# Issuing a kernel's first loads in the program's first block, ahead of the entry barrier

## The chip, the cores and the metric

The kernel runs on one core of one Trainium2 chip. The metric is the device time of one execution in microseconds (us). A profile of one execution gives the span of the core, which is 1.3 to 1.8 us shorter than the device time in the runs here, and the record of each instruction and of each DMA packet. The time axis of a profile starts at the first recorded instruction.

Abbreviations of the profile: PE is TensorE (matmul), PEld its weight loads, DVE VectorE, ACT ScalarE, POOL GpSimd, SP SyncE. A "q" behind a name (SPq) is that engine's instruction sequencer, which also issues DMAs.

## The reference

One decoding step: pre-layernorm attention over a cache of 4096 keys, 32 heads, batch 4, then a dense block with a Mish activation. Everything is bf16.

```python
def _A_ref(x, k_cache, v_cache, wq, wo):            # x: 4 x 1 x 640
    q = (x @ wq).reshape(4, 1, 32, 128)...          # k_cache, v_cache: 4 x 32 x 4096 x 128
    scores = jnp.einsum("bhqd,bhkd->bhqk", q, k_cache) * (128 ** -0.5)
    p = _softmax(scores, axis=-1)
    o = jnp.einsum("bhqk,bhkd->bhqd", p, v_cache)
    return o...reshape(4, 1, 32 * 128) @ wo

h  = x + _A_ref(_layernorm(x), k_cache, v_cache, wq, wo)
h2 = h + _B_ref(_layernorm(h), w1, b1, w2)          # w1: 640 x 1728, b1: 1728, w2: 1728 x 640
```

The two caches are 268 MB, and each byte is used once.

## The kernel before

The work is cut into 16 tiles (`NT`) of 8 heads of one batch entry. A K tile and a V tile are 8 MB each. There are three big buffers, slots A, B and C; K tiles go to A and B, V tiles to C and A. wq sits in slot C at first, the later weights go into A and B at the end. SP issues nearly all loads; ScalarE issues four small ones. Each engine's program is written out with its own semaphore waits (`need`).

These are the loads that the change moves:

```python
    def first_loads():
        load(
            sp, slot["C"][:, 0 : DC * H * Dh], A_wq.rearrange("(p c) n -> p (c n)", c=DC), "wq", "WQ"
        )                                                            # 5 MB
        load(ac, x_bf[:, :], x_rows[:, :], "x", "X")                 # 5 KB
        load(ac, w2_tail[0:FT, :], B_w2[FM * P : F, :], "w2t", "WT") # 80 KB: rows 1664 to 1727 of w2
        k_load(0)                                                    # 8 MB into slot A
        k_load(1)                                                    # 8 MB into slot B
```

The end of SP's program and the start of ScalarE's, which the argument needs too:

```python
    def sync_prog():
        ...                                  # K and V tiles, each when its slot comes free
        sp.need(("F", NT - 1, NS - 1))       # slot B free
        for n, (q, j0, j1) in enumerate(WOS):
            load(sp, wo_sb[:, q, j0:j1, :], ..., ("wo", q, j0), f"W{n}")    # five pieces
        for k, (c0, c1) in enumerate(zip(W1S, W1S[1:])):
            load(sp, w1_sb[:, c0:c1, :], ..., ("w1", c0), ...)              # three pieces
        sp.need(("PV", NT - 2))              # slot A free
        for k, (j0, j1) in enumerate(zip(W2S, W2S[1:])):
            load(sp, w2_sb[:, j0:j1, :], ..., ("w2", j0), ...)              # four pieces
        ...
    def act_prog():
        ac.need("b1z")
        load(ac, b1T[:, 0:FM], ..., "b1a", "S")              # 3.2 KB, runs of 26 bytes
        load(ac, b1T[0:FT, FM : FM + 1], ..., "b1b", "S")    # 0.1 KB, runs of 2 bytes
        ...
```

And how the program is put together. Ahead of all this stands a first block, "main": four small memsets on GpSimd, then on each engine a drain and a semaphore wait that together make the entry barrier, then a branch to the next block.

```python
    with tc.tile_critical(name="k", no_gpsimd_drain=True):
        first_loads()
    tc.close()
    tc.compile()
    for p, f in progs:
        f()
        if p is po:
            clear()
```

The softmax here doesn't subtract the row's maximum and nothing guards it: scores larger than these inputs give would overflow.

Of the kernel before, what the change touches and what calls it, by code (L numbers as in the profile page):

```python
# [78 lines left out]
def kernel(  # L79
# [13 lines left out]
    nc = tc.nc  # L93
# [155 lines left out]
    def load(p, dst, src, key, sem):  # L249
        p.do(lambda: p.eng.dma_start(out=dst, in_=src), key, sem, 16)  # L250
# [15 lines left out]
    def clear():  # L266
        fin = book.handles["FIN"]
        nc.gpsimd.wait_ge(fin, 2).then_inc(fin, -2)
        nc.clear_and_free_semaphores(
            [h for k, h in book.handles.items() if k not in ("OUT0", "OUT1", "FIN")]  # L270
        )

    def k_load(i):
        c = KS[i % N]
        load(sp, slot[c][:, :], tiles(A_k_cache, i), ("K", i), "K" + c)
# [11 lines left out]
# [4 lines that stand above are left out]
        load(ac, x_bf[:, :], x_rows[:, :], "x", "X")  # L291
        load(ac, w2_tail[0:FT, :], B_w2[FM * P : F, :], "w2t", "WT")
        k_load(0)
        k_load(1)
# [654 lines left out]
    book.ready = True  # L949
    for p, f in progs:  # L950
        p.restart(True)
    with tc.tile_critical(name="k", no_gpsimd_drain=True):
        first_loads()
    tc.close()
    tc.compile()
    for p, f in progs:
        f()
        if p is po:
            clear()
# [30 lines left out]
```

## Time and profile before

The time before is 663.92 us (median of 3 runs, 663.88 to 663.99). What matters of its profile:

| quantity | value |
|---|---|
| span | 662.2 us |
| bytes in SP's DMA queue | 283.27 MB |
| share of that queue's packets in sixteen DMA engines' span | 99.0% |
| VectorE, TensorE busy | 61%, 60% |
| SP's first DMA issue | 0.95 us |
| first packet of that queue (packet records) | 1.96 us |
| last weights packet (packet records) | 658.1 us |

The queue table of before follows; its columns are packets, megabytes and share of sixteen engines' span. q1 is SP's queue, q10 ScalarE's; "..." marks lines left out, here and in all fences below.

```profile
q1 hardware_dynamic: 6640, 283.27, 99.0%
...
q10 hardware_dynamic: 328, 0.09, 0.1%
```

The first microseconds of before, from the timeline. The columns are start in us, duration in us, then the engine, source line and operation; the bracket is the idle time before it and what ended it.

```profile
0.90 0.56 ACTq L250 DMA_DIRECT2D x_bf<-in_A_x_dram  x1
0.95 0.40 SPq L250 DMA_DIRECT2D slotC<-in_A_wq_dram  x1
...
1.50 0.53 ACTq L250 DMA_DIRECT2D w_tail<-in_B_w_dram  x1
...
3.38 0.20 POOL L335 MEMSET ident<- 128x128 bf16 x1 [2.93 <-POOLq L955]
...
3.45 0.88 DVE L441 BATCH_NORM_STATS2 stats<-x_bf 4x6 f32<-4x320 bf16 x2
...
16.97 4.46 PE L708 MATMUL red<-slotC,lnT 128*32 128x512 bf16 x40 [8.54 <-PEq L49]
...
36.84 4.43 DVE L515 TENSOR_TENSOR slotA<-slotA,q_bc 128x8192 bf16<-128x8192 bf16 x1 [28.68 <-DMA slotA<-in_A_k_cache_dram]
```

SP could not issue before 0.95 us. TensorE had nothing to do between the end of its setup, about 8.4 us, and 16.97 us, when wq had landed. SP's own waits in before say what it stood at (columns: microseconds in total, times, longest); line 974 is the entry barrier:

```profile
SPq L974 <- PEq L974: 0.7, 1, 0.7
SPq L955 <- PEq L955: 0.5, 2, 0.3
```

The chain of waits of before, its first pieces in order of time (start, duration, what): it starts at the second half of the last V tile. "issue" is time in which the engine waited for nothing that the profile shows.

```profile
635.98 0.04 issue
636.02 3.60 PE pv L708 x30
639.62 1.69 PE y_ps L708 x40
...
645.90 1.55 PE y_ps L708 x40
647.46 0.04 issue
647.50 1.75 PE y_ps L708 x40
```

### The profile page before, as it was taken

How to read it: one execution, taken by the hardware profiler on the slowest of the kernel's cores; microseconds unless marked ns; L12 is line 12 of the kernel's file. 1: busy time of each engine (PE TensorE's matmuls, PEld its weight loads, DVE VectorE, ACT ScalarE, POOL GpSimd, SP SyncE). 2: the span in 40 equal slices, each digit the busy share in tenths (PEclk: the TensorE clock that was granted, in tenths of full speed). 3: DMA queues.
4: the chain of work that ended last, by engine and by line, in shares of the span. 5: the costliest groups of instructions: out<-in, count | busy, mean ns of one | idle time of the engine just before them, and what ended most of it. 6: DMA issues, size and time to landing. Idle time of an engine off the chain costs nothing. (4 is left out here: it accounts for less than half of the span.)

```text
span 662.2 us, 5205 instructions
## 1 busy us (share of the span) xinstructions
PE 399.4 (60%) x2747; PEld 83.3 (13%) x1787; DVE 406.8 (61%) x252; ACT 41.6 (6%) x158; POOL 2.6 (0%) x14
## 2 busy tenths in 40 slices
PE   0957666557317595838307485828534757675877
PEld 0710010101101010101100010100110001010147
DVE  1067889486048778677219688948306798858612
ACT  0110000000000000000000000000000000000011
POOL 1000000000000000000000000000000000000000
PEclk9998698869659796869668778977965879786855
DMA  9999999999999999999999999999999999999997
GB/s 385 437 443 413 420 444 433 444 435 436 421 432 439 428 443 435 439 420 435 439 428 435 443 439 420 435 439 424 439 439 443 420 435 435 428 439 439 412 419 289
DMA packets 6978, 283.50 MB, mean 428 GB/s; under 512 B 1012, under 2 KB 1208, under 8 KB 2232
## 3 DMA queue, kind: packets, MB, share of 16 engines
q1 hardware_dynamic: 6640, 283.27, 99.0%
q8 instruction: 7, 0.11, 0.1%
q10 hardware_dynamic: 328, 0.09, 0.1%
q14 instruction: 3, 0.02, 0.0%
HBM read 283.35 MB, written 0.01 MB: 428 GB/s over the span
## 5 line engine op out<-in xcount | busy, mean ns | idle before, releaser
L515 DVE TENSOR_TENSOR slotA<-slotA,q_bc 128x8192 bf16<-128x8192 bf16 x32 | 140.6, 4415 | 108.1 <-DMA slotA<-in_A_k_cache_dram 108.1
L515 DVE TENSOR_TENSOR slotB<-slotB,q_bc 128x8192 bf16<-128x8192 bf16 x32 | 140.7, 4417 | 17.0 <-DMA slotB<-in_A_k_cache_dram 17.0
L526 DVE TENSOR_REDUCE s_f<-red 128x64 f32<-128x1024 f32 x64 | 78.0, 1219 | 97.6 <-PE red L718 97.6
L718 PE MATMUL red<-slotA,ident 128*128 128x512 bf16 x480 | 135.9, 446 | 0.0
L718 PE MATMUL red<-slotB,ident 128*128 128x512 bf16 x480 | 127.9, 426 | 0.0
L708 PE MATMUL red<-slotA,ident 128*128 128x512 bf16 x32 | 14.3, 447 | 117.2 <-PEq L49 117.2
L708 PE MATMUL pv<-slotC,e 128*32 128x512 bf16 x768 | 53.1, 437 | 37.0 <-PEq L49 34.0
L708 PE MATMUL red<-slotB,ident 128*128 128x512 bf16 x32 | 14.1, 441 | 87.7 <-PEq L49 87.7
L394 ACT ACTIVATE ex<-s_f 128x64 bf16<-128x64 f32 x64 | 16.4, 256 | 503.2 <-DVE s_f L526 503.2
L540 DVE TENSOR_TENSOR e<-ex,hmask 128x512 bf16<-128x512 bf16 x64 | 39.8, 683 | 0.0
L708 PEld LDWEIGHTS pv<-slotC,e 128*32 128x32 bf16 x768 | 22.7, 108 | 94.1 <-issue 80.5
L708 PEld LDWEIGHTS red<-slotA,ident 128*128 128x128 bf16 x32 | 3.2, 99 | 184.7 <-issue 184.6
L708 PEld LDWEIGHTS red<-slotB,ident 128*128 128x128 bf16 x32 | 3.2, 99 | 171.9 <-issue 171.9
L708 PEld LDWEIGHTS o_ps<-pv_sb,selo 128*32 128x32 f32 x136 | 13.9, 113 | 65.0 <-issue 64.8
L708 PE MATMUL o_ps<-pv_sb,selo 128*32 128x128 f32 x136 | 18.9, 284 | 0.0
L708 PE MATMUL pv<-slotA,e 128*32 128x512 bf16 x256 | 14.6, 380 | 0.3 <-PEq L49 0.3
L404 ACT COPY pv_sb<-pv 128x512 f32<-128x512 f32 x16 | 9.4, 586 | 68.4 <-PE pv L708 68.4
L708 PE MATMUL red<-q_all,sel 32*128 32x128 bf16 x128 | 12.5, 307 | 0.8 <-PEq L49 0.8
L708 PEld LDWEIGHTS red<-q_all,sel 32*128 32x128 bf16 x128 | 12.2, 142 | 1.7 <-issue 1.7
L394 ACT ACTIVATION_READ_ACCUMULATOR ex<-s_f 128x1 f32 x64 | 11.9, 186 | 0.0
L708 PEld LDWEIGHTS pv<-slotA,e 128*32 128x32 bf16 x256 | 6.7, 97 | 23.4 <-issue 17.5
L708 PE MATMUL red<-slotC,lnT 128*32 128x512 bf16 x40 | 4.5, 629 | 8.5 <-PEq L49 8.5
(96 smaller groups left out, 74.3 us busy)
## 6 DMA issues: line engine op xcount, KB each, us to landing
slotC<-in_A_v_cache_dram SPq DMA_DIRECT2D x2, 4096.0 KB, 39.1
slotC<-in_A_wq_dram SPq DMA_DIRECT2D x1, 5120.0 KB, 15.9
slotB<-in_A_wo_dram SPq DMA_DIRECT2D x3, 1280.0 KB, 15.7
slotB<-in_B_w_dram SPq DMA_DIRECT2D x2, 864.0 KB, 22.8
slotB<-in_A_wo_dram SPq DMA_DIRECT2D x1, 960.0 KB, 20.1
slotA<-in_B_w_dram SPq DMA_DIRECT2D x1, 960.0 KB, 25.1
slotA<-in_B_w_dram SPq DMA_DIRECT2D x1, 640.0 KB, 22.3
slotB<-in_B_w_dram SPq DMA_DIRECT2D x1, 432.0 KB, 24.2
```

Of the source, the lines that this page charges most:

```text
L394: lambda: a.activation(out=ex[:, sl], in_=s_f[:, sl], func=ACT.Exp, scale=SCALE, accum_out=rs[:, b, s : s + 1],),
L404: lambda: a.copy(out=pv_sb[:, :, :].rearrange("p r d -> p (r d)"), in_=pv[:, :]),
L515: lambda: v.tensor_tensor(out=t, in0=t, in1=q_bc[:, hg, b, :].unsqueeze(1).to_broadcast([P, RS, Dh]), op=ALU.mult,),
L526: lambda: v.tensor_reduce(out=s_f[:, s * RS : (s + 1) * RS], in_=red[:, k : k + 2, :].rearrange("p k (r c) -> p (k r) c", c=CW), axis=AX.X ...
L540: lambda: v.tensor_tensor(out=e[:, sl, :], in0=ex[:, sl].unsqueeze(2).to_broadcast([P, RS, G]), in1=hmask[:, :].unsqueeze(1).to_broadcast( ...
L708: lambda: nc.tensor.matmul(out_, lhsT=lhsT, rhs=rhs, start=start, stop=stop, skip_group_check=skip),
L718: return t.add_instruction(mybir.InstMatmult(name=nc.get_next_instruction_name(), engine=mybir.EngineType.PE, ins=[t.lower_ap(rhs), t.lowe ...
```

## The change

The intent is to start the stream of loads sooner. The five first loads leave the critical section (`tile_critical`, a block that the other engines wait behind), which is dropped. They are issued after the program has been compiled, cut out of the block they fell into, and put into the block "main", on each engine just ahead of its drain, so that no barrier stands before them.

```diff
     for p, f in progs:
         p.restart(True)
-    with tc.tile_critical(name="k", no_gpsimd_drain=True):
-        first_loads()
     tc.close()
     tc.compile()
+    here = nc.cur_bb.bb
+    n = len(here.instructions)
+    first_loads()
+    moved = here.instructions[n:]
+    here.instructions = here.instructions[:n]
+    main = nc.bb_map["main"].bb
+    order = main.instructions
+    for ins in moved:
+        place = next(
+            k for k, o in enumerate(order) if o.engine == ins.engine and isinstance(o, mybir.InstDrain)
+        )
+        order = order[:place] + [ins] + order[place:]
+    main.instructions = order
     for p, f in progs:
         f()
```

## The prediction

> **What bounds the kernel now.** The SP DMA queue. Its packets take 99.0% of sixteen engines' span (queue table): 283.27 MB, mean 428 GB/s (DMA summary). In the packet records at least one packet of that queue is in flight at every moment from about 2.0 to 658.1 us, without a gap over 50 ns. VectorE is 61% and TensorE 60% busy, and VectorE's longest wait is for K tiles (108.1 us in four waits, waits table). The steady slices run at up to 444 GB/s; "DMA: Bandwidth & Descriptors" of the Trainium skill (section Specifications) puts the fabric ceiling at 435 GB/s, and this trace agrees within 2%. So transfers can't be made faster; they can start earlier. The chain of waits is the last 24 us of compute (636.0 to 660.3 us), which starts when the second half of the last V tile has landed, so it hangs on the stream too. The last weights land at 658.1 us, 1.9 us before the last matmul ends.
>
> **What the change does.** Timeline of the first 4 us: SP's first instruction, its drain, is at 0.00 us; it waits 0.7 us for the entry barrier (SP's wait table), passes a no-op and a branch, and issues wq at 0.95, K tile 0 at 1.40, K tile 1 at 1.87 us (0.40 to 0.42 us each). The first packet follows the first issue by 1.0 us. ScalarE's drain is at 0.14, its first issue at 0.90 us. After the change these issues stand ahead of the drain: SP should issue wq at about 0.0, ScalarE x at about 0.14 us. The critical section goes, with its branches, no-ops and two further barriers, which now let the compute engines begin at 3.4 us.
>
> Added: the entry barrier waits until SP has issued three transfers, 3 x 0.42 + 2 x 0.06 = 1.4 us, so the engines start at about 1.8 us (estimate from these durations), still 1.6 us sooner. That is off the critical path: TensorE finishes its setup at 8.4 us and waits until 16.94 us for wq.
>
> **How much is on the critical path.** Only the 0.95 us by which SP's first issue moves. Nothing should eat it: the queue is never empty later, since tiles are issued one or two ahead (27 to 45 us from issue to landing), and the releases that trigger them come from landings and shift with them. The matmuls on wq should start at 16.0 instead of 16.94, the first multiply at 35.9 instead of 36.84, the chain at 635.1 instead of 636.0; the span goes from 662.2 to 661.2.
>
> The tail runs at a granted clock of 0.50 from 630.5 us on. The clock changes in steps of 3.41 us; by "TensorE: Matmul & The Clock Gate" (section What's actually happening) that window is free-running, so a shift under 1 us lands nowhere in particular on it. Three runs of before agree within 0.11 us: I expect no luck from there.
>
> **Prediction.** 663.92 - 0.95 = 662.97 us, say 663.0; eight in ten between 662.3 and 663.8. Faster by over 2%: 0.005; within 2%: 0.99; slower: 0.005.
>
> **What would show it.** Right: SP issues at 0.0 / 0.45 / 0.9 us; first packet at about 1.05 us; VectorE's first instruction near 1.8 us; first matmul on wq near 16.0 us; unchanged GB/s in steady slices; a tail of 24 us. Wrong: an unchanged first packet (queue not ready earlier); a gap in the DMA records later; a longer tail, or one at another clock.
>
> **What would make it wrong.** The measured time starts at an event that moves with SP's first instruction; the first issue takes longer when nothing precedes it; the start-up takes HBM or fabric time from something else; the tail's clock flips.

## The result and the profile after

The changed kernel took 662.85 us (median of 4 runs, 662.62 to 663.05) against 663.90 us of before (4 runs, 663.63 to 663.99). The ratio of the two is 0.9985 with a 95% interval of 0.9967 to 1.0002; a ratio is computed as the mean time of one kernel's fast runs over that of the other's of the same rounds, so it is not quite the ratio of the medians. That interval includes 1. A second measurement with five rounds (below, after_again) gave 0.9985 again, interval 0.9972 to 0.9999, a difference of means of 1.01 us. The change is worth about 1.0 us, 0.15%.

The queue table of after: the same packets, in a shorter span.

```profile
q1 hardware_dynamic: 6640, 283.27, 99.2%
...
q10 hardware_dynamic: 328, 0.09, 0.1%
```

The first microseconds of after:

```profile
0.00 0.40 SPq L250 DMA_DIRECT2D slotC<-in_A_wq_dram  x1
0.12 0.56 ACTq L250 DMA_DIRECT2D x_bf<-in_A_x_dram  x1
...
0.73 0.55 ACTq L250 DMA_DIRECT2D w_tail<-in_B_w_dram  x1
...
2.60 0.20 POOL L335 MEMSET ident<- 128x128 bf16 x1 [2.16 <-POOLq L953]
...
5.51 0.88 DVE L441 BATCH_NORM_STATS2 stats<-x_bf 4x6 f32<-4x320 bf16 x2 [2.78 <-DMA x_bf<-in_A_x_dram]
...
16.02 4.42 PE L708 MATMUL red<-slotC,lnT 128*32 128x512 bf16 x40 [6.80 <-PEq L49]
...
36.20 4.42 DVE L515 TENSOR_TENSOR slotA<-slotA,q_bc 128x8192 bf16<-128x8192 bf16 x1 [27.27 <-DMA slotA<-in_A_k_cache_dram]
```

SP issues wq at 0.00 us, and the matmuls on wq start 0.95 us sooner, at 16.02 us. Two things are not as one would guess. The compute engines begin at 2.6 us (GpSimd's line 335), only 0.8 us sooner. And VectorE's first work on x starts at 5.51 us, 2.06 us later than in before, because it waits for x. VectorE's first multiply on a K tile moved by 0.64 us only, from 36.84 to 36.20 us; more on that at the end.

SP's waits in after:

```profile
SPq L953 <- PEq L953: 0.5, 2, 0.3
SPq L985 <- PEq L985: 0.2, 1, 0.2
```

The two barriers of 0.5 us in total are still there: their line, 955 in before and 953 in after, is that of `tc.compile()`, not of the critical section.

The chain of waits of after now names a transfer where that of before named matmuls:

```profile
615.65 0.04 issue
...
624.24 22.11 DMA slotB<-in_A_wo_dram
646.35 0.14 issue
646.49 1.75 PE y_ps L708 x40
```

The piece of wo that lands last but one releases TensorE's last 40 matmuls on wo. The semaphore records of the two traces give the landings (us), the moments at which a transfer's last completion signal arrives, which the chain of before hid:

| landing | before | after | sooner by |
|---|---|---|---|
| wq | 16.83 | 15.88 | 0.95 |
| second half of the last V tile | 635.89 | 634.89 | 1.00 |
| wo, third piece | 645.04 | 644.08 | 0.96 |
| wo, fourth piece | 647.36 | 646.35 | 1.01 |
| last piece of w2 | 658.40 | 657.52 | 0.88 |
| start of the last 40 matmuls on wo | 647.50 | 646.49 | 1.01 |

In both kernels those 40 matmuls start 0.14 us after the fourth piece of wo has landed. It is 0.13 or 0.14 us in the trace of every other run that loads wo in these pieces, too. In before TensorE came to that point at 647.46 us, 0.04 us earlier than it could go on, so the chain was followed along the matmuls. In after TensorE happened to be granted more of its clock (0.78 against 0.50 between 636 and 642 us), came sooner and waited. It gained nothing by it.

### The profile page after: what moved, and what is told of

Read it like the earlier page. It is cut to its first block, busy times and chain, and to the rows that moved or that the text cites. A ratio compares the mean times of both kernels' runs of the same rounds, so it can differ in the third digit from the quotient of the medians.

```text
span 661.1 us, 5195 instructions
## 1 busy us (share of the span) xinstructions
PE 396.9 (60%) x2747; PEld 80.8 (12%) x1787; DVE 406.9 (62%) x252; ACT 41.6 (6%) x158; POOL 2.6 (0%) x14
## 5 line engine op out<-in xcount | busy, mean ns | idle before, releaser
L708 PE MATMUL red<-q_all,sel 32*128 32x128 bf16 x128 | 10.3, 273 | 0.8 <-PEq L49 0.8
L708 PEld LDWEIGHTS red<-q_all,sel 32*128 32x128 bf16 x128 | 10.1, 124 | 1.6 <-issue 1.6
```

The costliest lines, as they stand in the source:

```text
L708: lambda: nc.tensor.matmul(out_, lhsT=lhsT, rhs=rhs, start=start, stop=stop, skip_group_check=skip),
```

## The experiments

Each kernel ran five rounds against before. "Over before" is the mean of its five runs less the mean of nine runs of before; its standard error, worked out from the spread of those runs, is 0.09 to 0.23 us. The changed kernel was repeated in one of these calls only (after_again); kernels of other calls are compared with it through before. By the interval of the ratio all of these kernels count as the same as before (the measure there is 2%); the differences of interest are tenths of a microsecond, and what carries them is that they line up with the packet records.

| run | first packet of SP's queue, us | median, us | over before, us | standard error, us |
|---|---|---|---|---|
| before | 1.96 | 663.74 to 663.94 | 0 | |
| after_again | 1.02 | 662.97 | -1.01 | 0.09 |
| sp_only | 1.03 | 663.01 | -1.03 | 0.15 |
| delay_1 | 1.88 | 663.86 | -0.22 | 0.17 |
| no_critical | 2.41 | 664.40 | +0.68 | 0.23 |
| act_only | 3.16 | 664.44 | +0.53 | 0.15 |
| delay_2 | 3.10 | 664.45 | +0.67 | 0.15 |
| delay_2_again | 3.10 | 664.40 | +0.62 | 0.20 |
| delay_2_late | 3.10 | 665.01 | +1.13 | 0.12 |
| delay_4 | 7.24 | 668.59 | +4.91 | 0.16 |
| tail_split | 1.03 | 663.27 | -0.67 | 0.20 |
| w2t_tail | 1.02 | 662.65 | -1.23 | 0.19 |
| w2t_b1_tail | 1.02 | 661.96 | -2.00 | 0.15 |

The theory: the stream of SP's queue is the bound, and the time follows the start of that stream. Rival A: the gain comes from the critical section and its barriers that went, or from compute engines that start sooner. Another rival: the gain is chance, such as the clock in the tail.

### after_again: the changed kernel, measured again

No edit.

> The changed kernel once more, with five rounds, as the yardstick for the other runs on this chip. Stream theory (the SP queue's stream is the bound and only its start counts): 1.0 us faster than before (ratio 0.9985), as SP's first issue moves from 0.95 to 0.00 us. Rival (the gain was the granted clock of the tail in one execution, or noise): less than 0.4 us.

Measured: 1.01 us faster than before, five runs within 0.15 us. In its profile the fourth piece of wo landed at 646.69 us and the chip granted the tail 0.50 of the clock, as in before; the gain in time was the same. That speaks against the clock as its cause. (That landing is 0.34 us later than in after, from the same first packet: single executions differ by this much, so it is the means that count.)

### sp_only: SP's loads ahead of the barrier, ScalarE's not

```diff
+    with tc.tile_critical(name="k", no_gpsimd_drain=True):
+        first_act()                      # x and w2's last rows, on ScalarE
     tc.close()
     tc.compile()
     here = nc.cur_bb.bb
     n = len(here.instructions)
-    first_loads()
+    first_sp()                           # wq and two K tiles, on SP
```

> SP's three loads stand ahead of the entry barrier, ScalarE's two loads stay in the critical section behind it. Stream theory: SP issues at 0.0 us, the whole gain stays, 1.0 us faster than before, 662.9 us; x is issued at about 2 us, lands near 7 us behind the packets of wq, and TensorE's setup ends near 11 us, which costs nothing because wq lands at 15.9 us. Rival A (the gain is the critical section and its barriers, or the sooner start of the compute engines): most of the gain is lost, 663.6 to 664 us.

Its first microseconds, from the timeline:

```profile
0.00 0.41 SPq L250 DMA_DIRECT2D slotC<-in_A_wq_dram  x1
...
1.99 0.56 ACTq L250 DMA_DIRECT2D x_bf<-in_A_x_dram  x1
...
8.55 0.88 DVE L447 BATCH_NORM_STATS2 stats<-x_bf 4x6 f32<-4x320 bf16 x2 [4.09 <-DMA x_bf<-in_A_x_dram]
...
15.93 4.46 PE L714 MATMUL red<-slotC,lnT 128*32 128x512 bf16 x40 [3.68 <-PEq L49]
```

Measured: 1.03 us faster than before, so the whole gain. The critical section is back, the compute engines begin later than in before, and VectorE gets x only at 8.55 us, 5.1 us later than in before. None of that costs anything. Rival A falls. It is also shown that the late x of the changed kernel is harmless: TensorE's setup ended at 12.25 us here, and wq landed at 15.79 us.

### act_only: ScalarE's loads ahead of the barrier, SP's not

The same split, with `first_act()` moved into "main" and `first_sp()` in the critical section.

> Only ScalarE's two loads stand ahead of the entry barrier, SP's three stay in the critical section. Stream theory: SP issues wq at 1.0 to 1.3 us (the barrier now waits for ScalarE's two issues and its drain, so perhaps later than in before), so no gain, or a loss of up to 1 us: 663.8 to 664.9 us, and the difference from before equals the difference of the first issue. Rival A (an earlier x and an earlier setup): up to 1 us faster than before.

```profile
0.13 0.56 ACTq L250 DMA_DIRECT2D x_bf<-in_A_x_dram  x1
...
2.14 0.40 SPq L250 DMA_DIRECT2D slotC<-in_A_wq_dram  x1
...
4.56 0.87 DVE L447 BATCH_NORM_STATS2 stats<-x_bf 4x6 f32<-4x320 bf16 x2
```

Measured: 0.53 us slower than before. The direction is that of the theory: SP's first issue went from 0.95 to 2.14 us, since the barrier waits for ScalarE's two issues. But the size isn't: the first packet came 1.20 us later and the time grew by less than half of that. This miss led to the delay runs.

### delay_1, delay_2, delay_4: the changed kernel with a late start

Drains on SP, which do nothing else here, hold up its first load; the rest of the change stays. (The rule for the place had to name the block's own drain, as there are more drains now.)

```diff
+    for _ in range(16):                  # 40 in delay_2, 80 in delay_4
+        nc.sync.drain(fusable=False)
     first_loads()
```

> The changed kernel with sixteen drains on SP in front of its first load, at about 60 ns each about 0.95 us: the first issue is back where it was before, everything else of the change stays (no critical section, ScalarE's loads early). Stream theory: the gain is gone, 663.9 us, within 0.2 us of before, although x lands early. Rival A (the missing critical section and its barriers): the gain stays, 662.9 us.

> The changed kernel with forty drains on SP in front of its first load (sixteen took 0.84 us, so forty about 2.1 us). In act_only the first issue was 1.19 us later than in before, yet the time only 0.5 us longer, where the stream theory said about as much as the issue moved. Stream theory with slope one: 2.1 us over the changed kernel, 665.1 us. Rival B (a part of a later start is given back, by transfers of ScalarE that then run ahead of the stream, or by slack later): the same as act_only, which has the same first issue, 664.5 us. If it is 665.1, act_only owes its difference to something else than the first issue.

> The same with eighty drains, about 4.2 us. Stream theory with slope one: 667.2 us, 4.2 over the changed kernel. Rival B with a fixed amount given back once (about 0.6 us): 666.6. Rival B with a share given back (a slope of about 0.7): 666.0 us.

Measured: delay_1, whose first packet came within 0.08 us of where it came in before, is back at the time of before, within the error (-0.22 us), although it has no critical section. (VectorE's first work on x was at 3.32 us, against 3.45 in before.) That is the second blow to rival A. delay_2 has the first packet of act_only and its time too (+0.67 and +0.53 us), so what act_only owed didn't lie in the critical section. With delay_4 the time grew nearly with the start again: first packet +5.28 us, time +4.91. So an amount of about 0.4 to 0.7 us (0.67 in act_only, 0.47 in delay_2, 0.37 in delay_4) had been given back once, not a share of the delay.

One thing in delay_4 was not planned: its first issue took 2.00 us in place of 0.40, so that the first packet was later than the 80 drains alone make it. Why is open; the comparison uses the packet's measured time.

```profile
4.62 2.00 SPq L250 DMA_DIRECT2D slotC<-in_A_wq_dram  x1
```

### delay_2_again and delay_2_late: what was given back

The packet records offered a candidate. In act_only, delay_2 and delay_4 all 68 packets of ScalarE's first two loads (x and w2's last rows) went through before the first packet of SP's queue. In before, after and sp_only at most 3 of them did. delay_2_late is delay_2 with the 80 KB load put behind the barrier:

```diff
     def first_loads():
         ...
         load(ac, x_bf[:, :], x_rows[:, :], "x", "X")
-        load(ac, w2_tail[0:FT, :], B_w2[FM * P : F, :], "w2t", "WT")
         ...
     def act_prog():
         a = nc.scalar
+        load(ac, w2_tail[0:FT, :], B_w2[FM * P : F, :], "w2t", "WT")
         ac.need("b1z")
```

> The kernel of delay_2 once more, as the yardstick for the next run, and to see whether its time holds: 0.5 to 0.8 us over before, where the first packet of the stream (3.10 us against 1.96) says 1.14 us.

> delay_2 with one load put back: ScalarE's 80 KB of w2's last rows are issued behind the entry barrier, when the stream already runs, in place of ahead of it. In delay_2 and act_only, where all 68 packets of ScalarE's first two loads went before the first packet of the stream (0.28 us of all sixteen engines), the time was 0.4 to 0.6 us less than the first packet's shift says. If those packets are what was saved: 0.2 to 0.5 us slower than delay_2, about 1.0 us over before. If the saving has another cause (slack further down, the chip's spread): the same as delay_2.

```profile
0.74 0.53 ACTq L250 DMA_DIRECT2D w_tail<-in_B_w_dram  x1
2.07 0.40 SPq L250 DMA_DIRECT2D slotC<-in_A_wq_dram  x1
```

```profile
2.07 0.40 SPq L250 DMA_DIRECT2D slotC<-in_A_wq_dram  x1
...
4.49 0.53 ACTq L250 DMA_DIRECT2D w_tail<-in_B_w_dram  x1
```

The first fence is delay_2, the second delay_2_late: only the order of the two loads differs. Measured: delay_2_again +0.62 us over before, delay_2_late +1.13 us, which is the 1.14 us by which its first packet is later than that of before. The load beside the stream costs 0.5 us (1.13 less 0.65, the mean of the two runs of delay_2). Its 81,920 bytes are only 0.19 us at the mean rate of 428 GB/s. The traces place this cost: from the first packet to wq's landing the stream took 15.01 us in delay_2_late and 14.26 and 14.12 us in the two runs of delay_2, and to the landing of K tile 0 35.16 against 34.49 and 34.60 us. With that, act_only's miss (0.67 us, with an error of 0.15) is explained within the errors.

### no_critical: no critical section, nothing moved ahead

The loads are issued plainly after `tc.compile()`, behind the entry barrier and the two barriers of the next block; the lines that move them are dropped.

> The five first loads are issued without a critical section, but behind the entry barrier, in the block after it; nothing is moved ahead. Before's branches and no-ops of the critical section are gone, two barriers at the start of the next block stand ahead of the loads. Stream theory: SP's first issue at 1.4 to 1.7 us, and the time follows it: 0.4 to 0.8 us slower than before, 664.4 to 664.8 us. Rival A (removing the critical section is what pays): faster than before, 663 to 663.5 us.

Measured: SP's first issue at 1.39 us, first packet 0.45 us later than in before, time +0.68 us with an error of 0.23. Removing the critical section alone does not help, although GpSimd begins its work at 1.39 us here, 2 us sooner than in before; the sign is that of the later start, and so is the size within the error. The third test against rival A.

### tail_split: smaller last pieces of wo and w1

In after TensorE waited for wo's fourth piece, so smaller pieces might release it sooner.

```diff
-    WOS = [(k, 0, G) for k in range(NHG - 1)] + [(NHG - 1, 0, G - 2), (NHG - 1, G - 2, G)]
-    W1S = (0, 2, DC - 1, DC)
+    WOS = [(k, 0, G) for k in range(NHG - 1)] + [(NHG - 1, j, j + 2) for j in range(0, G, 2)]
+    W1S = tuple(range(DC + 1))
```

> The changed kernel with the last quarter of wo loaded in four pieces in place of two, and w1 in five in place of three. In the changed kernel TensorE waited for the first of those two pieces until 646.35 us, and the tail after it took 12.9 us, while the last weights had landed at 657.5 us. If the tail hangs on pieces landing, matmuls on the first pieces can start sooner: 0.3 to 0.6 us faster than the changed kernel, 662.4 to 662.7 us. If the tail's own length or the issue of more transfers bounds it: no gain, or a loss of some tenths.

Measured: -0.67 us over before, so no better than the changed kernel's -1.01, within the errors perhaps worse (0.20 and 0.09). Its runs scatter over 0.95 us. A miss; whether the smaller pieces cost anything is not settled. That little could be won is seen in other traces: at a granted clock of 0.50 (before, after_again) TensorE had ended the work before those 40 matmuls only 0.03 to 0.04 us before it started them, while in after, with more clock, it was 0.55 us.

### w2t_tail and w2t_b1_tail: take the small loads off the stream's path

If 80 KB beside the stream cost 0.5 us of it, they had better not be there. The tail is released by wo, and what comes behind wo in SP's queue has some slack. w2t_tail lets SP issue the last rows of w2 behind w1, and w2t_b1_tail also moves the two loads of b1, to between wo and w1.

```diff
     def first_loads():
         ...
-        load(ac, w2_tail[0:FT, :], B_w2[FM * P : F, :], "w2t", "WT")
     def sync_prog():
         ...                              # the five pieces of wo
+        sp.need("b1z")                                           # w2t_b1_tail only
+        load(sp, b1T[:, 0:FM], ..., "b1a", "S")                  # w2t_b1_tail only
+        load(sp, b1T[0:FT, FM : FM + 1], ..., "b1b", "S")        # w2t_b1_tail only
         ...                              # the three pieces of w1
+        load(sp, w2_tail[0:FT, :], B_w2[FM * P : F, :], "w2t", "WT")
         sp.need(("PV", NT - 2))
     def act_prog():
-        ac.need("b1z")                                           # w2t_b1_tail only
-        load(ac, b1T[:, 0:FM], ..., "b1a", "S")                  # w2t_b1_tail only
-        load(ac, b1T[0:FT, FM : FM + 1], ..., "b1b", "S")        # w2t_b1_tail only
```

> The changed kernel with the 80 KB of w2's last rows taken out of the start: SP issues them in its own queue after w1, where they no longer stand ahead of the wo pieces that release the tail. delay_2_late showed that this load, run beside the stream, costs 0.5 us (1.13 against 0.65 us over before). If it is the load's place ahead of wo's landing that costs: 0.3 to 0.5 us faster than the changed kernel, 1.3 to 1.5 us faster than before. If the bytes cost the same wherever they run: as the changed kernel, 1.0 us faster than before.

> The same with the two b1 loads (192 packets of 26 and 2 bytes, 0.11 us of sixteen engines) also moved into SP's queue, after wo and ahead of w1. Expected: 0.1 us faster than w2t_tail, or, if the small packets hold up w1's landing, up to 0.3 us slower than it.

Measured: w2t_tail is 1.23 us faster than before. Against the changed kernel's 1.01 that is 0.2 us with an error of the same size: inconclusive alone. w2t_b1_tail is 2.00 us faster than before (ratio 0.9970, interval 0.9956 to 0.9983): 661.96 us, its five runs from 661.84 to 662.42. All five are below all nine runs of the changed kernel, the lowest of which is 662.62. It beats both kernels. Its chain of waits has the shape of before's, only earlier:

```profile
634.43 3.60 PE pv L708 x32
...
645.87 0.06 issue
645.92 1.75 PE y_ps L708 x40
```

The fourth piece of wo landed at 645.78 us, 0.57 us sooner than in after, and the 40 matmuls behind it started at 645.92. The size of the second step was missed: 0.1 us had been expected of the b1 loads, from the time of their own 192 packets, and the difference of the two kernels is 0.77 us (2.00 less 1.23, with an error of about 0.2). The 3.4 KB of b1, issued by ScalarE beside the stream, held up wo by far more than their own packets' time. The traces place this too: from wq's landing to that of K tile 0 the stream took 20.36 us in w2t_tail, where b1's packets ran from 6.84 to 32.70 us, and 19.53 us in w2t_b1_tail. The 0.77 us was measured with the 80 KB already out of the way; what moving b1 alone would give, with the 80 KB left in place, is not measured. And the stream as a whole did not get shorter: its last weights packet ended at 657.14 us in after as in w2t_b1_tail. What was won is that wo, which releases the tail, lands sooner, and that the rest had slack. How the small loads hold up the stream is not shown: no run tells the ways apart.

## Why the prediction was right

The prediction was 662.97 us and the result 662.85 us, inside the range of 662.3 to 663.8.

- **The bound.** Right. The time followed the first packet of SP's queue: -0.94 us gave -1.0, -0.08 gave -0.22 (error 0.17), +1.14 gave +1.13 where ScalarE's load stayed beside the stream as in before. The landings of wq, of the last V tile and of wo moved by 0.95 to 1.01 us.
- **"The first multiply at 35.9."** Missed: it came at 36.20 us, 0.64 us sooner in place of 0.95. K tile 0 landed 20.22 us after wq in after and 19.90 us in before, so a third of the gain was gone there; it came back when before lost 0.3 us on one tile between 94 and 114 us. In both kernels most tiles landed 19.3 us after the one before, 8.39 MB at 435 GB/s, so the steady rate was unchanged as forecast. But a single tile takes 0.1 to 0.5 us longer in one run or another, and why is open. So it is in part luck that these two profiles show a shift of 1.01 us at wo, within 0.06 us of the forecast; the means of five runs are what carries the result.
- **The 0.95 us.** Right, and right for the stated reason: sp_only, which moves SP's issues alone, has the whole gain. The issues were at 0.00, 0.46 and 0.92 us where 0.0, 0.45 and 0.9 had been written, and the first packet at 1.02 us where 1.05 had been.
- **"two further barriers" would go, engines start at 1.8 us.** Wrong. The two barriers stay (0.5 us in SP's waits in both kernels), and the drains behind the issues, which the estimate took for nothing, took 0.32 us on SP and 0.39 us on ScalarE in after's trace. The engines began at 2.6 us. It didn't matter, since that step was off the critical path, as said.
- **x.** Not foreseen. SP's first issue now comes 0.12 us before ScalarE's, while in before x was issued 0.05 us before wq. x's packets got in behind wq's first packets of 40 KB each; the 19 of those that started before the first packet of x took 1.5 to 3.0 us each. The first packet of x was at 3.24 us, where in before it was at 1.85. VectorE waited for x until 5.51 us. sp_only shows that even 8.55 us is harmless. TensorE's setup ended at 9.22 us, where it had ended at 8.43: had it been on the critical path, this order would have turned the gain into a loss of about 0.8 us (an estimate from these two). "DMA: Bandwidth & Descriptors" of the Trainium skill (section Queues, rings and completion order) says that a DMA engine takes turns between queues packet by packet, whole packets at a time; these records agree: each of x's four packets starts within 5 ns of the end of one of wq's first sixteen.
- **The chain "hangs on the stream".** Right in substance, and the place was off: what releases the tail is not the last V tile but the fourth piece of wo, 11 us later. In before the two paths met within 0.04 us, and the chain showed only one of them; the prediction read the tail off that chain.
- **The tail's clock.** The prediction had listed a tail at another clock as a sign against it. In after's profile the last 24 us were granted 0.57, in before's 0.50. It made no difference, as wo's landing set the pace, and after_again had the gain at 0.50.
- **"Nothing should eat it."** Right for the gain, but the account was not complete: the small loads of ScalarE hold up the stream by more than the time of their bytes. In after they take as much as in before, so it did not show; it showed when act_only and delay_2 took them out.

## What to carry to other kernels

In this kernel, whose DMA queue is busy from its first packet to its last weights, the time follows the start of that queue, and moving the first issue ahead of the entry barrier was worth what the barrier held it up, no more; what the compute engines win at the start was worth nothing while they waited for the first load. Look then for small loads on other queues that run beside the stream: put behind the load that releases the tail, 83 KB of them gave as much again as the change. And a chain of waits shows one path where two may tie: compare the landings of the transfers in both traces before you say what released a stage.

## What the Trainium skill lacked or had wrong

- "DMA: Bandwidth & Descriptors" (section Rules for kernel authors) says that with many transfers under 64 KB one pays mostly overhead, but not what a small load costs a large stream on another queue. Here an 80 KB load beside the stream cost 0.5 us, where its bytes at 428 GB/s are 0.19 us; and moving 3.4 KB in 192 packets of 26 and 2 bytes behind wo in the stream's own queue gave 0.77 us, where their packets' own time is 0.11 us of sixteen engines.
- The same page (section Latency and other measured facts) gives about 600 ns to the first byte for DMAs issued by SP or ScalarE, and does not say from when. In after the first packet came 1.02 us after the start of the issuing instruction, 0.61 us after its end.
- "VectorE: DVE Perf Modes" (section The DRAIN you can't avoid) describes the drains that frame a kernel as constant, about 12 ns. The drains of this program's entry barrier, which may or may not be the ones that it means, took 7 ns on SP and 8 ns on ScalarE in before; right behind DMA issues, in after, they took 319 and 387 ns, and the barrier came behind them.
- No page that I found tells what a program's own entry barrier costs the first DMA: SP waited 0.7 us at it in before, and its first issue was at 0.95 us.
